# Retention attention followed by a GELU MLP on one core: the first unit's v over SyncE's queue, attention visits timed to TensorE's instruction pieces, and a new order of loads

## The chip, the core and the metric

The kernel runs on one core of a Trainium2 chip. TensorE (PE in the profile) multiplies, VectorE (DVE), ScalarE (ACT) and GpSimd (POOL) do the elementwise work, and the queues of SyncE (SP), ACT and POOL issue transfers to 16 shared DMA engines. The metric is the device time of one execution in microseconds; less is better.

## The reference

Inputs are q, k and v, each 8 x 8 x 576 x 64 fp32 (batch, heads, positions, width of a head), and two weights. The first part is attention without a softmax: each score is damped by a power of the head's gamma.

```python
scores = scale * np.matmul(q, k.transpose(0, 1, 3, 2))
Dmat = np.where(rel >= 0, gamma[:, None, None] ** rel[None, :, :], 0.0)
ret = scores * Dmat[None, :, :, :]
attn_out = np.matmul(ret, v)
x = attn_out.transpose(0, 2, 1, 3).reshape(4608, 512)
h = x @ w_in                      # w_in 512 x 2048
g = 0.5 * h * (1.0 + erf(h / sqrt(2)))
out = g @ w_out                   # w_out 2048 x 512
```

## The kernel before

**Units and visits.** The 576 positions are cut into chunks of 128 and a tail of 64. A unit is one chunk of one batch element with all 8 heads (the two tails of a pair of batch elements share one unit); there are 36. Units 0 to 3 stand alone, later chunks go in groups of two. A group passes these steps on PE: its q and k are transposed (`turn`, L421, by PE; from group 8 on `turn_dve`, L441, by DVE); a visit called S makes the scores (`scores`, L473, L488 to L506), and DVE multiplies them by the damping (`masked`, L527 to L533, tile `ret`); a visit called A (`attend`) multiplies by v (`inner`, L558 to L569), updates the state that a chunk hands to the next (`state`, U, L584, L589) and adds what the state before gives (`cross`, L646). DVE or ACT then writes the result into `x` (L669, L383). The first visit A, of unit 0, reads v as it was loaded.

**The MLP.** Four units make a block of 512 tokens; there are 9 blocks. `mlp1` (L689, tile `hT`) is the first product, followed by GELU on ACT into `g_all`; `mlp2` (L722, tile `oT`) is the second for half of block 0. The rest of the second product, and the first product of blocks 6 to 8, use Strassen-like schemes of seven products in place of eight (`mlp2_fast`, L793, tiles `fa`, `fb`; `mlp1_fast`, L897, tiles `ha`, `hb`), whose sums and differences DVE makes (`g_sum`, L761; the sums of the weights, L748 and L862).

**What sets the order.** The Python program is a planner. It keeps a clock for each engine in `T`, estimated landing times in `land`, and in its main loop picks the next piece of PE work: a due U, A, S or transposition first, else a step of the MLP. Dummy products (`warm`, L1112 and L1139) fill waits in the first 16 us. Loads come from the list `ORDER`, which POOL's queue issues one after the other (`load`: L322 for q, k, v, L278 for pieces of `w_in`, L293 for pieces of `w_out`); these convert fp32 to bf16 on the way, and eight semaphores go round, so that POOL holds back a load while the eighth before it is under way. After the list, `reload` adds loads as units are finished. Only unit 0's q and k come over SP's and ACT's queues (L132), as fp32, and are cast by DVE or ACT (L381, through `cast_due`). Constants of the planner: `RATE` bounds how far attention runs ahead of the MLP's block number, `SB` how much planned DVE work may be ahead when a visit S is let in, `PER_B` weighs the MLP's sums against attention's jobs on DVE, `STORE_AT` is the earliest time of block 0's stores, `CROWD` the time up to which a store is planned to delay loads, `STATE10` the earliest time of the state of units 2 and 3. In the planner as it stands, PE's clock knows nothing of the fetching of instructions.

Below are the functions that the diff touches and what calls them.

Of the kernel before, what the change touches and what calls it, by code (L numbers as in the profile page):

```python
# [17 lines left out]
def kernel(  # L18
# [72 lines left out]
    HK = N_DF // 2  # L91
# [181 lines left out]
    def load(what, i):  # L273
        if what == "io":
            constants()
            return
        if what == "wi":
            nc.gpsimd.dma_start(w_in[:, :, i * 256:(i + 1) * 256],  # L278
                                moe_w_in[:, i * 256:(i + 1) * 256].rearrange("(c p) f -> p c f", p=128))
            land_in[i] = sw_dma(0.75, 1.33)  # L280
            return
# [34 lines left out]
        for jj in (j,) if j is not None else range(2):  # L316
# [3 lines left out]
            else:  # L320
# [47 lines left out]
    def release(b, when):  # L368
        held.remove(b)
        free_at[b] = when  # L370

    def pe(dur, to="full"):
# [42 lines left out]
    def turn(n, jj, half):  # L415
        qk, dst = loaded[groups[n][0]][0][jj], turned(n, jj)
        b, t = bank([128, HP, 128], BF16, "qk_ps")
        rows = TAIL if units[groups[n][0]][2] is None else C
        for x in range(HP):
            what = qk[:, 2 * x:2 * x + 2, :] if n < 4 else qk[0:rows, HP * half + x, :, :]  # L420
            nc.tensor.transpose(t[:, x, 0:rows], what, ident[0:rows, 0, 0:rows])  # L421
# [42 lines left out]
    def scores(n):  # L464
# [3 lines left out]
        if n < 4:  # L468
            got = [bank([128, HP, 128], FP32, "sc") for _ in range(2)]
            for hp in range(HP):  # L470
                for e in range(2):
                    sl = slice(64 * e, 64 * e + 64)
                    nc.tensor.matmul(got[e][1][:, hp, :], lhsT=kT[sl, hp, :], rhs=qT[sl, hp, :],  # L473
                                     start=True, stop=True)
            st[g[0]]["sc"] = got, pe(0.23, "row")
        elif n in BY_DVE:
# [5 lines left out]
            for hp in range(HP):  # L482
                for y in range(2):
                    for e in range(2):
                        for j in range(2):
                            sl = slice(64 * e + 32 * j, 64 * e + 32 * j + 32)
                            dst = got[e][1][64 * j:64 * j + 64, hp, :] if short else got[j][e][1][:, hp, :]
                            nc.tensor.matmul(dst, lhsT=turned_k(n, sl, hp, y), rhs=turned_q(n, sl, hp, y),  # L488
                                             start=(y == 0), stop=(y == 1), skip_group_check=True)
# [3 lines left out]
        elif len(g) == 1:  # L493
            got = [bank([128, H, TAIL], FP32, "sc") for _ in range(2)]
            for h in range(H):
                for j in range(2):
                    sl = slice(64 * j, 64 * j + 64)
                    nc.tensor.matmul(got[j][1][sl, h, :], lhsT=kT[sl, h, :TAIL], rhs=qT[sl, h, :TAIL],
                                     start=True, stop=True)
            st[g[0]]["sc"] = got, pe(0.23, "quad")  # L500
        else:
            got = [[bank([128, HP, 128], FP32, "sc") for _ in range(2)] for _ in g]
            for h in range(H):
                for j in range(2):
                    sl = slice(64 * j, 64 * j + 64)
                    nc.tensor.matmul(got[j][h % 2][1][:, h // 2, :], lhsT=kT[sl, h, :], rhs=qT[sl, h, :],  # L506
                                     start=True, stop=True)
# [41 lines left out]
    def inner(i):  # L549
        bp, ci, j = units[i]  # L550
        s = st[i]
        if j is None:
            s["o"] = [bank([128, HP, TAIL], FP32, "o_ps") for _ in range(2)]
            for h in range(H):
                for jj in range(2):
                    sl, e = slice(64 * jj, 64 * jj + 64), 64 * (h % 2)
                    y = h // 2 + HP * (h % 2) if group_of[i] in BY_DVE else h
                    nc.tensor.matmul(s["o"][jj][1][e:e + 64, h // 2, :], lhsT=s["vh"][sl, h, :], rhs=s["ret"][0][sl, y, :],  # L558
                                     start=(h < 2), stop=False, skip_group_check=True)
            s["B"] = pe(0.25, "quad")  # L560
            s_done.add(i)
        else:
# [3 lines left out]
            for hp in range(HP):  # L566
                for z in range(4):
                    e, d0 = z // 2, z % 2 * 32
                    nc.tensor.matmul(o[32 * z:32 * z + 32, hp, :], lhsT=vals[:, 2 * hp + e, d0:d0 + 32], rhs=s["ret"][e][:, hp, :],  # L569
                                     start=(hp == 0), stop=(ci == 0 and hp == HP - 1), skip_group_check=True)  # L570
# [4 lines left out]
    def state(bp, ci):  # L575
        pair = pair_of[bp, ci]
        b, u_ps = bank([128, H, D], FP32, "u_ps")
        for hp in range(HP) if packed(pair[0]) else ():
            for y in range(2):
                for e in range(2):  # L580
                    for j, i in enumerate(pair):
                        h, p0 = 2 * hp + e, 64 * e + 32 * j
                        keys = loaded[i][0][1][:, h, y::2] if i < 4 else loaded[i][2][:, h, j, y::2]
                        nc.tensor.matmul(u_ps[p0:p0 + 32, 2 * hp + y, :], lhsT=keys, rhs=st[i]["vh"][:, h, :],  # L584
                                         start=(hp == y == 0), stop=(hp == HP - 1 and y == 1), skip_group_check=True)
        for h in range(H) if not packed(pair[0]) else ():
            for j, i in enumerate(pair):
                keys = loaded[i][0][1][:, h, :] if i < 4 else loaded[i][2][:, h, j, :]
                nc.tensor.matmul(u_ps[64 * j:64 * j + 64, h, :], lhsT=keys, rhs=st[i]["vh"][:, h, :],  # L589
                                 start=(h == 0), stop=(h == H - 1), skip_group_check=True)  # L590
# [36 lines left out]
    def cross(n):  # L627
# [7 lines left out]
        for hp in range(HP):  # L635
            for y in range(2) if by_dve else (None,):
                for e in range(2):
                    for j in range(2):
# [7 lines left out]
                        nc.tensor.matmul(o[64 * e:64 * e + 64, hp, :], lhsT=a, rhs=b_, start=False,  # L646
                                         stop=(hp == HP - 1 and y != 0), skip_group_check=True)
# [37 lines left out]
    def mlp1(t, m0, n, lo, hi):  # L685
        b, hT = bank([128, n, hi - lo], FP32, "hT")
        for m in range(m0, m0 + n):
            for cc in range(N_DM):
                nc.tensor.matmul(hT[:, m - m0, :], lhsT=w_in[:, cc, m * 128:m * 128 + 128], rhs=x_tiles[t][:, cc, lo:hi],  # L689
                                 start=(cc == 0), stop=(cc == N_DM - 1))  # L690
# [25 lines left out]
    def mlp2(t, ts, m0, m1):  # L716
# [4 lines left out]
        for m in range(m0, m1):  # L721
            nc.tensor.matmul(oT, lhsT=g_of(t, ts // 2)[:, m, cols], rhs=w_out[:, m, :], start=(m == 0), stop=(m == N_DF - 1))  # L722
        done = pe((m1 - m0) * 0.2158)
# [58 lines left out]
    def mlp2_fast(t, p, name):  # L782
# [9 lines left out]
        for kk in range(HK):  # L792
            nc.tensor.matmul(dst, lhsT=x[:, kk, :], rhs=y[:, kk, :], start=(name in "125" and kk == 0),  # L793
                             stop=(kk == HK - 1), skip_group_check=True)
# [85 lines left out]
    def mlp1_fast(t, i, name):  # L880
# [13 lines left out]
        for m in range(2):  # L894
            for cc in range(HC):
                c0 = (2 * i + m) * 128
                nc.tensor.matmul(dst[:, m, :], lhsT=a[cc][:, c0:c0 + 128], rhs=y[:, cc, :],  # L897
                                 start=(name in "125" and m == 0 and cc == 0), stop=(cc == HC - 1), skip_group_check=True)
# [210 lines left out]
    def warm(n):  # L1109
        b, t = bank([128, 512], FP32, "warm")  # L1110
        for _ in range(n):
            nc.tensor.matmul(t, lhsT=zeros[:, :128], rhs=zeros, start=True, stop=True)  # L1112
        pe((0.32 if T["pe"] < HOT else 0.2158) * n)
# [23 lines left out]
    for _ in range(N_WARM):  # L1137
        b, t = bank([128, 512], FP32, "warm")
        nc.tensor.matmul(t, lhsT=zeros[:, :128], rhs=zeros, start=True, stop=True)  # L1139
        release(b, 0.0)  # L1140
    T["pe"] = 1.3 + 0.62 * N_WARM
    while True:
# [16 lines left out]
        if nB < nA:  # L1159
# [109 lines left out]
```

## Time and profile before

| | |
|---|---|
| three runs, median (lowest to highest) | 292.16 us (291.55 to 292.23) |
| profiled execution, its own time | 292.13 us |
| its span | 290.3 us |
| outside the span | 1.83 us |
| PE busy | 284.0 us (98%), 3992 matmuls |
| DVE, POOL, ACT busy | 241.5, 159.4, 144.0 us |
| granted PE clock | 1.0 |
| PE's instructions, by their DMA queue q8 | 31 transfers of 16 KB |

A line of the timeline gives start, duration, engine, source line, operation, output<-input and, in brackets, how long the engine stood idle before it and what ended that. In the chain of waits each line is a piece of the path that ended last: start, duration, and what filled it. PE's busy time counts overlapping matmuls to their modelled ends, so that "busy" hides small gaps; spacings between starts show them. q8 carries PE's instructions in pieces of 16 KB: some 7,984 instructions (3992 weight loads and as many matmuls) in 31 pieces are 256 to a piece.

### The profile page before, as it was taken

How to read it: one execution, taken by the hardware profiler on the slowest of the kernel's cores; microseconds unless marked ns; L12 is line 12 of the kernel's file. 1: busy time of each engine (PE TensorE's matmuls, PEld its weight loads, DVE VectorE, ACT ScalarE, POOL GpSimd, SP SyncE). 2: the span in 40 equal slices, each digit the busy share in tenths (PEclk: the TensorE clock that was granted, in tenths of full speed). 3: DMA queues.
4: the chain of work that ended last, by engine and by line, in shares of the span. 5: the costliest groups of instructions: out<-in, count | busy, mean ns of one | idle time of the engine just before them, and what ended most of it. 6: DMA issues, size and time to landing. Idle time of an engine off the chain costs nothing.

```text
span 290.3 us, 9332 instructions
## 1 busy us (share of the span) xinstructions
PE 284.0 (98%) x3992; PEld 212.6 (73%) x3992; DVE 241.5 (83%) x445; ACT 144.0 (50%) x270; POOL 159.4 (55%) x232
## 2 busy tenths in 40 slices
PE   7999999999999999999999999999999999999995
PEld 2588677888874566666666676677888888888884
DVE  5581599789999999989983388999999998899962
ACT  7377333665346546555365544434545545543521
POOL 8975689999878898889799994300000000000000
PEclk9999999999999999999999999999999999999999
DMA  9999999999999999999999992002002101201013
GB/s 145 165 188 202 188 179 185 164 117 113 149 162 129 135 118 114 181 93 142 159 135 189 146 98 72 5 5 75 2 0 76 72 2 72 76 0 73 37 58 128
DMA packets 111418, 31.55 MB, mean 109 GB/s; under 512 B 89104, under 2 KB 107024, under 8 KB 111376
## 3 DMA queue, kind: packets, MB, share of 16 engines
q0 software_dynamic: 103744, 20.99, 85.0%
q1 hardware_dynamic: 6144, 9.18, 9.5%
q10 hardware_dynamic: 1488, 0.79, 1.0%
q8 instruction: 31, 0.51, 0.7%
q14 instruction: 11, 0.09, 0.1%
HBM read 42.47 MB, written 9.44 MB: 179 GB/s over the span
## 4 chain that ended last, share of the span: by engine, by line
PE 80%; DMA 9%; POOL 6%; DVE 4%; issue 1%; POOLq 0%; DVEq 0%
PE hT L689 23%; PE fa L793 19%; PE fb L793 14%; PE ha L897 7%; PE hb L897 5%; DMA w_out<-in_moe_w_out_dram 4%; DMA w_in<-in_moe_w_in_dram 3%; POOL early L322 3%; PE o_ps L569 3%; DMA qk_ld<-in_q_dram 3%; PE o_ps L646 2%; PE sc L488 2%; POOL w_in L278 2%; PE u_ps L584 1%; PE qk_ps L421 1%; DVE ret L533 1%
## 5 line engine op out<-in xcount | busy, mean ns | idle before, releaser
L689 PE MATMUL hT<-x,w_in 128*128 128x512 bf16 (+2 forms) x536 | 93.1, 319 | 0.1
L689 PEld LDWEIGHTS <-w_in 128*128 128x128 bf16 x536 | 48.8, 98 | 24.5 <-issue 0.3
L793 PEld LDWEIGHTS <-g_all 128*128 128x128 bf16 x544 | 52.3, 98 | 11.2 <-issue 1.1
L694 ACT ACTIVATE g_all<-hT 128x512 bf16<-128x512 f32 x64 | 38.2, 597 | 41.1 <-PE hT L689 41.1
L793 PEld LDWEIGHTS <-s 128*128 128x128 bf16 x408 | 39.6, 98 | 9.1 <-issue 0.6
L902 ACT ACTIVATE g_all<-t 128x512 bf16<-128x512 f32 x36 | 22.6, 630 | 32.9 <-DVE t L910 32.9
L306 POOL DMA_DIRECT2D k_ld<-in_k_dram x56 | 31.0, 568 | 8.5 <-DMA kn_ld<-in_k_dram 4.7
L533 DVE TENSOR_TENSOR ret<-sc,msk 128x512 bf16<-128x512 f32 x56 | 34.7, 681 | 1.0 <-PE sc L506 1.0
L779 DVE TENSOR_TENSOR o_sb<-fb,t 128x256 f32<-128x256 f32 x51 | 21.2, 418 | 17.1 <-ACT t L383 7.6
L793 PE MATMUL fa<-w_out,g_all 128*128 128x256 bf16 x272 | 35.1, 273 | 0.0
L322 POOL DMA_DIRECT2D v_ld<-in_v_dram x36 | 30.8, 858 | 2.5 <-DMA q_ld<-in_q_dram 1.4
L306 POOL DMA_DIRECT2D q_ld<-in_q_dram x56 | 31.1, 584 | 0.6 <-DMA qk_ld<-in_q_dram 0.6
L383 ACT COPY t<-fa 128x256 f32<-128x256 f32 x39 | 14.5, 371 | 29.5 <-PE fa L793 29.4
L910 DVE TENSOR_TENSOR t<-hb,t 128x512 f32<-128x512 f32 x36 | 24.7, 687 | 2.5 <-ACT t L383 1.5
L697 ACT ACTIVATE g_all<-hT 128x512 bf16<-128x512 f32 (+1 forms) x35 | 19.3, 560 | 10.8 <-PE hT L689 10.6
L669 DVE TENSOR_TENSOR x<-o_ps,dqT 128x512 bf16<-128x512 f32 (+1 forms) x36 | 20.9, 621 | 1.1 <-PE o_ps L646 1.1
L897 PEld LDWEIGHTS <-ws 128*128 128x128 bf16 x192 | 18.8, 98 | 2.5 <-issue 0.3
L312 POOL DMA_DIRECT2D kn_ld<-in_k_dram x22 | 19.9, 902 | 0.9 <-DMA q_ld<-in_q_dram 0.9
L793 PE MATMUL fb<-w_out,g_all 128*128 128x256 bf16 x136 | 17.7, 273 | 0.4 <-issue 0.4
L793 PE MATMUL fb<-w_out,s 128*128 128x256 bf16 x136 | 17.5, 273 | 0.3 <-DVE o_sb L779 0.3
L793 PE MATMUL fa<-wt,g_all 128*128 128x256 bf16 x136 | 17.5, 273 | 0.0
L793 PE MATMUL fa<-wt,s 128*128 128x256 bf16 x136 | 17.5, 273 | 0.0
(119 smaller groups left out, 453.0 us busy)
## 6 DMA issues: line engine op xcount, KB each, us to landing
out_dram<-o_sb SPq DMA_DIRECT2D x30, 256.0 KB, 2.8
v_ld<-in_v_dram POOLq DMA_DIRECT2D x28, 128.0 KB, 5.1
q_ld<-in_q_dram POOLq DMA_DIRECT2D x44, 64.0 KB, 4.4
k_ld<-in_k_dram POOLq DMA_DIRECT2D x44, 64.0 KB, 3.4
kn_ld<-in_k_dram POOLq DMA_DIRECT2D x22, 128.0 KB, 5.3
w_in<-in_moe_w_in_dram POOLq DMA_DIRECT2D x8, 256.0 KB, 6.9
w_out<-in_moe_w_out_dram POOLq DMA_DIRECT2D x8, 256.0 KB, 10.6
out_dram<-o_sb SPq DMA_DIRECT2D x7, 128.0 KB, 2.4
```

Source lines behind the costliest of these rows:

```text
L306: nc.gpsimd.dma_start(qk["qk".index(what)][p0:p0 + 32, 0:HP * per].rearrange("p (h x) -> p h x", h=HP), {"q": q, "k": k}[what][2 * bp + jj ...
L312: nc.gpsimd.dma_start(kn[:, :, j], k[2 * bp + j, :, ci * C:ci * C + C, :].rearrange("h s d -> s h d"))
L322: nc.gpsimd.dma_start(dst, src[2 * bp + jj, :, ci * C:ci * C + n, :].rearrange("h s d -> s h d"))
L533: nc.vector.tensor_tensor(r, t, by, op=ALU.mult)
L669: nc.vector.tensor_tensor(x[:, :, n * y:n * y + n], o, dqT[:, :, ci * C:ci * C + n], op=ALU.mult)
L689: nc.tensor.matmul(hT[:, m - m0, :], lhsT=w_in[:, cc, m * 128:m * 128 + 128], rhs=x_tiles[t][:, cc, lo:hi], start=(cc == 0), stop=(cc == N ...
L694: nc.scalar.activation(g_all[:, t % 2, :, m0, :], hT.rearrange("p n (a c) -> p (n a) c", a=2), AF.Gelu)
L779: nc.vector.tensor_tensor(dst, src, f[key], op=ALU.add)
L793: nc.tensor.matmul(dst, lhsT=x[:, kk, :], rhs=y[:, kk, :], start=(name in "125" and kk == 0), stop=(kk == HK - 1), skip_group_check=True)
L897: nc.tensor.matmul(dst[:, m, :], lhsT=a[cc][:, c0:c0 + 128], rhs=y[:, cc, :], start=(name in "125" and m == 0 and cc == 0), stop=(cc == HC ...
L902: nc.scalar.activation(g_of(t, part)[:, m0:m0 + 2], src, AF.Gelu)
L910: nc.vector.tensor_tensor(f[key], f["b"][1], f[key], op=ALU.add)
```

## The change

1. Unit 0's v is loaded at the start over SP's queue, behind q, as fp32 into a third tile (`first_v`), and cast like q and k through `cast_due`, with a planned landing at 7.45 us. The entry `v0` of `ORDER` then does nothing.
2. Every matmul and transposition goes through `mm` or `mm_turn`, which count PE's instructions. `pe()` notes when the count passes into a new piece of 256 and delays PE's planned clock if the piece before was passed less than `FETCH` = 5.0 us ago. `fetch_at` holds back visits A (192 instructions) and S (64) from group 4 on that would run into the next piece sooner than that.
3. `ORDER` is new in its first three quarters, and seven constants differ.

```diff
-    RATE = 4.6
-    STORE_AT = 48.0
-    CROWD = 66.0
-    STATE10 = 24.0
+    RATE = 3.8
+    STORE_AT = 58.0
+    CROWD = 40.0
+    STATE10 = 20.0
     HOT = 7.5
-    SLACK, SB, PER_G, PER_B, TURN0 = 1.6, 9.0, 6.0, 40.0, 3.0
+    FETCH = 5.0
+    SLACK, SB, PER_G, PER_B, TURN0 = 1.6, 12.0, 6.0, 30.0, 3.0
...
+    V0_HW = 1
...
-    for nm, src, eng in (("q32", q, nc.sync), ("k32", k, nc.scalar)):
+    for nm, src, eng in (("q32", q, nc.sync), ("k32", k, nc.scalar), ("first_v", v, nc.sync))[:2 + V0_HW]:
...
+        if what == "v" and i == 0 and V0_HW:
+            return
...
+    if V0_HW:
+        land["v", 0] = 7.45
...
-    ORDER = ("wi0 io k2 k1 v1 q1 v0 wi1 q2 q3 k3 wi4 v2 wi6 v3 wi7 wi5 wo2 wi3 wi2 wo0 wo3 wo1 wo6 k4 wo4 wo5 wo7 "
-             "q5 q4 k5 k6 q6 k7 v4 v5 q7 v8 v7 k9 dq2 v6 v9 q9 k8 q8 dq3 q11 v11 k10 q10 q12 dq4 v10 k12 n12 v12 "
+    if V0_HW:
+        cast_due["v", 0] = (loaded[0][1], first["first_v"])
+    ORDER = ("wi0 io k1 v1 q1 k2 wi1 q2 v0 wi4 q3 k3 v2 wi6 wo0 v3 wi5 wi7 wo2 wi3 wi2 wo3 wo6 wo1 k4 wo4 wo5 k5 "
+             "wo7 q5 q4 q6 k7 v4 k6 v5 q7 v8 v7 q9 k9 dq2 q8 v6 v9 k8 dq3 q11 v11 n12 k10 q12 k12 q10 dq4 v10 v12 "
              "n11 dq0 k11").split()
...
+    count = [3.0, 3.0]
+    piece = [0.0]
+
+    def mm(*a, **k):
+        count[0] += 2.004
+        nc.tensor.matmul(*a, **k)
...
+    def place(n):
+        return (n - 194.0) // 256, (n - 194.0) % 256
+
+    def fetch_at(n):
+
+        at = place(count[0])[1]
+        wait = piece[0] + FETCH - (256 - at) * 0.0075 if at + n >= 256 else 0.0
+        return 0.0 if T["pe"] < 20.0 else wait
...
     def pe(dur, to="full"):
...
-        T["pe"] += dur * (2.0 if T["pe"] < HOT else 1.0)
+        dur *= 2.0 if T["pe"] < HOT else 1.0
+        new, old = place(count[0])[0], place(count[1])[0]
+        if new > old:
+            turn_at = T["pe"] + dur * (1 - place(count[0])[1] / max(1.0, count[0] - count[1]))
+            wait = max(0.0, piece[0] + FETCH - turn_at) if T["pe"] > 20.0 else 0.0
+            piece[0] = turn_at + wait
+            T["pe"] += wait
+        count[1] = count[0]
+        T["pe"] += dur
...
-            acts.append((max(ready, free_time(out_banks(g))), "A"))
+            acts.append((max(ready, fetch_at(192 if n >= 4 else 0), free_time(out_banks(g))), "A"))
...
-                acts.append((max(sg[n]["T"], free_time(2 * len(g))), "S"))
+                acts.append((max(sg[n]["T"], fetch_at(64 if n >= 4 else 0), free_time(2 * len(g))), "S"))
```

More of the change, by code (lines that the diff above doesn't have):

```diff
@@ L370, in release, with mm_turn, one_piece @@
         free_at[b] = when
+    count = [3.0, 3.0]
[3 more added lines that the diff above has]
+        nc.tensor.matmul(*a, **k)
+    def mm_turn(*a, **k):
+        count[0] += 2.004
+        nc.tensor.transpose(*a, **k)
+    def place(n):
[4 more added lines that the diff above has]
+        return 0.0 if T["pe"] < 20.0 else wait
+    def one_piece(n):
+        return place(count[0])[1] + n < 512
     def pe(dur, to="full"):
@@ L420, in turn @@
             what = qk[:, 2 * x:2 * x + 2, :] if n < 4 else qk[0:rows, HP * half + x, :, :]
-            nc.tensor.transpose(t[:, x, 0:rows], what, ident[0:rows, 0, 0:rows])
+            mm_turn(t[:, x, 0:rows], what, ident[0:rows, 0, 0:rows])
         done = pe(0.225)
@@ L472, in scores @@
                     sl = slice(64 * e, 64 * e + 64)
-                    nc.tensor.matmul(got[e][1][:, hp, :], lhsT=kT[sl, hp, :], rhs=qT[sl, hp, :],
+                    mm(got[e][1][:, hp, :], lhsT=kT[sl, hp, :], rhs=qT[sl, hp, :],
                                      start=True, stop=True)
@@ L497, in scores @@
                     sl = slice(64 * j, 64 * j + 64)
-                    nc.tensor.matmul(got[j][1][sl, h, :], lhsT=kT[sl, h, :TAIL], rhs=qT[sl, h, :TAIL],
+                    mm(got[j][1][sl, h, :], lhsT=kT[sl, h, :TAIL], rhs=qT[sl, h, :TAIL],
                                      start=True, stop=True)
@@ L505, in scores @@
                     sl = slice(64 * j, 64 * j + 64)
-                    nc.tensor.matmul(got[j][h % 2][1][:, h // 2, :], lhsT=kT[sl, h, :], rhs=qT[sl, h, :],
+                    mm(got[j][h % 2][1][:, h // 2, :], lhsT=kT[sl, h, :], rhs=qT[sl, h, :],
                                      start=True, stop=True)
@@ L557, in inner @@
                     y = h // 2 + HP * (h % 2) if group_of[i] in BY_DVE else h
-                    nc.tensor.matmul(s["o"][jj][1][e:e + 64, h // 2, :], lhsT=s["vh"][sl, h, :], rhs=s["ret"][0][sl, y, :],
+                    mm(s["o"][jj][1][e:e + 64, h // 2, :], lhsT=s["vh"][sl, h, :], rhs=s["ret"][0][sl, y, :],
                                      start=(h < 2), stop=False, skip_group_check=True)
@@ L568, in inner @@
                     e, d0 = z // 2, z % 2 * 32
-                    nc.tensor.matmul(o[32 * z:32 * z + 32, hp, :], lhsT=vals[:, 2 * hp + e, d0:d0 + 32], rhs=s["ret"][e][:, hp, :],
+                    mm(o[32 * z:32 * z + 32, hp, :], lhsT=vals[:, 2 * hp + e, d0:d0 + 32], rhs=s["ret"][e][:, hp, :],
                                      start=(hp == 0), stop=(ci == 0 and hp == HP - 1), skip_group_check=True)
@@ L645, in cross @@
                             a, b_ = u[sl, 2 * hp + e, :], turned(n, 0)[sl, 2 * hp + e, cols]
-                        nc.tensor.matmul(o[64 * e:64 * e + 64, hp, :], lhsT=a, rhs=b_, start=False,
+                        mm(o[64 * e:64 * e + 64, hp, :], lhsT=a, rhs=b_, start=False,
                                          stop=(hp == HP - 1 and y != 0), skip_group_check=True)
@@ L688, in mlp1 @@
             for cc in range(N_DM):
-                nc.tensor.matmul(hT[:, m - m0, :], lhsT=w_in[:, cc, m * 128:m * 128 + 128], rhs=x_tiles[t][:, cc, lo:hi],
+                mm(hT[:, m - m0, :], lhsT=w_in[:, cc, m * 128:m * 128 + 128], rhs=x_tiles[t][:, cc, lo:hi],
                                  start=(cc == 0), stop=(cc == N_DM - 1))
@@ L721, in mlp2 @@
         for m in range(m0, m1):
-            nc.tensor.matmul(oT, lhsT=g_of(t, ts // 2)[:, m, cols], rhs=w_out[:, m, :], start=(m == 0), stop=(m == N_DF - 1))
+            mm(oT, lhsT=g_of(t, ts // 2)[:, m, cols], rhs=w_out[:, m, :], start=(m == 0), stop=(m == N_DF - 1))
         done = pe((m1 - m0) * 0.2158)
@@ L792, in mlp2_fast @@
         for kk in range(HK):
-            nc.tensor.matmul(dst, lhsT=x[:, kk, :], rhs=y[:, kk, :], start=(name in "125" and kk == 0),
+            mm(dst, lhsT=x[:, kk, :], rhs=y[:, kk, :], start=(name in "125" and kk == 0),
                              stop=(kk == HK - 1), skip_group_check=True)
@@ L1111, in warm @@
         for _ in range(n):
-            nc.tensor.matmul(t, lhsT=zeros[:, :128], rhs=zeros, start=True, stop=True)
+            mm(t, lhsT=zeros[:, :128], rhs=zeros, start=True, stop=True)
         pe((0.32 if T["pe"] < HOT else 0.2158) * n)
@@ L1138 @@
         b, t = bank([128, 512], FP32, "warm")
-        nc.tensor.matmul(t, lhsT=zeros[:, :128], rhs=zeros, start=True, stop=True)
+        mm(t, lhsT=zeros[:, :128], rhs=zeros, start=True, stop=True)
         release(b, 0.0)
```

8 lines of the change are left out of this document (4 added, 4 removed).

## The prediction

> **What bounds the kernel now.** First the page's busy times and its chain of waits:
>
> ```profile
> PE 284.0 (98%) x3992; PEld 212.6 (73%) x3992; DVE 241.5 (83%) x445; ACT 144.0 (50%) x270; POOL 159.4 (55%) x232
> PE 80%; DMA 9%; POOL 6%; DVE 4%; issue 1%; POOLq 0%; DVEq 0%
> ```
>
> PE is the bound, but 15% of the chain is POOL and DMA. The same chain in order of time shows where:
>
> ```profile
> 2.65 4.37 POOL early L322 x5
> 7.01 0.75 POOL w_in L278
> 7.77 2.63 POOL early L322 x3
> ...
> 15.74 9.03 DMA w_in<-in_moe_w_in_dram
> 25.05 10.60 DMA w_out<-in_moe_w_out_dram
> ...
> 37.77 7.36 DMA qk_ld<-in_q_dram
> 45.18 1.07 PE qk_ps L421 x16
> ```
>
> Up to 45.18 us the end is set by POOL issuing loads one by one, then by transfers; from there PE leads. The third view, the timeline, shows the start of PE and POOL and two later places where PE stands still:
>
> ```profile
> 6.10 0.91 POOL L322 DMA_DIRECT2D early<-in_v_dram  x1
> 7.77 3.85 PE L1112 MATMUL warm<-zeros 128*128 128x512 bf16 x10
> 12.43 0.41 PE L569 MATMUL o_ps<-ret,early 128*32 128x128 bf16 x16
> ...
> 139.71 1.03 PE L689 MATMUL hT<-x,w_in 128*128 128x512 bf16 x4
> 141.15 1.05 PE L793 MATMUL fb<-w_out,g_all 128*128 128x256 bf16 x8 [0.42 <-issue]
> ...
> 178.28 1.03 PE L793 MATMUL fb<-w_out,s 128*128 128x256 bf16 x8 [0.28 <-DVE o_sb L779]
> ```
>
> The first visit A waits for v0, fifth in POOL's queue, while PE runs dummies. At 141.15 PE waits for nothing that the profile names; in the queues' view a transfer of q8 (PE's instructions) lies between 138.1 and 140.0. Four hT there took 1.44 us from start to next start, 0.87 elsewhere: 0.57 lost. The fourth view, busy time by stage, says what runs beside PE:
>
> ```profile
> 60.00:100.00 40.00, 40.00 (x773) 29.06 (x772) 39.16 (x66) 21.73 (x39) 35.59 (x57) 1.00 1.39 136
> 100.00:140.00 40.00, 40.00 (x765) 26.28 (x763) 38.25 (x65) 20.39 (x37) 36.56 (x57) 1.00 1.37 131
> ```
>
> The columns are PE, weight loads, DVE, ACT, POOL: from 60 to 140 us DVE is full too (39.2 and 38.3 of 40).
>
> **The change, part by part.** The sum is made against the profiled execution's 292.13 us (span 290.3, 1.83 around it), 0.03 under the median.
>
> *v0 off POOL's queue.* It removes one of ten issues of L322 in the chain (5+3+1+1), 4.37/5 = 0.87 to 0.91 us; what follows v0 up to q7, the load that ends the chain at 45.18, moves by 0.9. Can PE follow? v0 being there by 8, A0 can run near 9.4 instead of 12.43, and q1 (now fourth of POOL's loads) comes 0.9 earlier; then by 14.4 PE can have done, over what it has now, the second visit A (0.34 from start to next start), the first state (0.38) and three more first products of 128 tokens (0.45 each): 2.07, say 2.0 us, for which the dummies (3.85 us at 7.77) make room. But PE then reaches the end of its work sooner: the eight products of oT end at 38.84, and by the trace's semaphores the last piece of w_out, which they need, lands at 36.65. In the new order k5 goes before it (+0.9) and v0 is gone (-0.9), so it stays, and oT can end no earlier than 36.65 + 0.86 (four 0.216 us products) = 37.5, 1.3 before now. Ends: -2.0 (all of PE's early work kept) and 0 (transfers alone set the chain). I take -0.9, the POOL row, between oT's -1.3 and 0.
>
> *v0 on SP's queue.* 256 KB as fp32; q, alike, lands in 3.6 us, at 4.3; k on ACT at 4.9. The three move at 204 to 288 GB/s in the timeline of transfers, so v0 costs the DMA engines 262 KB / 0.25 = 1.05 us, POOL's bf16 v0 131 KB / 0.16 = 0.8. Net +0.2; ends 0 and +1.05, if k and the first w_in come later by all of it. A late k delays the transposes of 5.70, covered by the dummies; without them 1.05. The cast (0.43, row of q's) falls into DVE's idle 0.77 before 7.94. SP's issue (0.44) is ahead of nothing: its first store is at 39.
>
> *Pieces.* Visits that would run into the next piece are held back. Seen stalls: 0.57 at 141; the other visible waits of PE after 45 name DMA (0.3) or DVE (0.3). Ends: -1.5 (unnamed starts of 0.1 after some 15 visits in one) and 0. I take -0.57, the row. The hold itself stops nothing on PE, since the planner issues an MLP step instead; behind the held visit wait DVE's ret and x and the next state. At the worst it is 5.0 - 192 x 0.0075 = 3.56 us after a turn of pieces; in 100 to 200 us PE has a block or more of second product in hand (14 products of 0.87 = 12 us), so it costs 0 there. Without that cover it costs what it holds. The Trainium skill (Runtime: NRT & Kernel Launch, Instruction fetch mechanics) says that the sequencer fetches the next block of 256 instructions while it executes the current one, and that this is mostly hidden; by it the term is 0 and the sum -0.7, by the row -0.57 and -1.27. The trace agrees in 30 of 31 pieces, not at 141.
>
> *Orders and constants.* wo0 comes 6 places earlier (one piece, some 1.3 us of transfer, ahead of v3, wi5, wi7); PE has hT to do at 20 to 32 (64 products from 25.79): 0. k2 later: needed only with q2. State (1,0) at 20: its 0.35 us of PE are only moved. Stores at 58: two o_sb of four stay held from 39, the next second product starts at 68: 0, and loads from 48 to 58 have less beside them. RATE: at 122 us attention is at unit 24 and the MLP at block 3.56, where the limit was 32.4 and is 29.5: not reached. SB and PER_B change DVE's order; S behind A saves PE a change of shape (32 `sc` take 0.38 at 95.91, 0.56 at 84.47, so 0.18), and there are 14 such visits: five more or fewer of these savings are -0.9 to +0.9, I take 0.
>
> Sum: -0.9 + 0.2 - 0.57 = -1.27: 290.86, so 290.9.
>
> **The rivals.** *All of PE's start is kept* (289.1): -2.0 in place of -0.9, pieces -0.57, the 0.44 at 178 (1.31 against 0.87 for four hT) and the 0.26 at 45 go, with the +0.2 it is -3.07. For it: PE waits 3.85 us in dummies. Against: w_out's landing allows 1.3.
>
> *DVE takes it back* (291.6). DVE writes block 2's x from 83.64 to 84.90, and its first hT starts at 84.98, behind a visit S, just as block 1's second product runs out. A PE that is 0.7 earlier by 60 would stand there unless DVE, full since 60, is earlier as well; DVE idles 2.7 us from 50 to 60, which speaks for it. Only the pieces stay: 292.13 - 0.57.
>
> *Slower: DVE's queue* (293.9). SB lets a visit S in behind 12 planned us of DVE work instead of 9, so one more visit's four ret (2.48 us at 171.99) can stand ahead of sums that the second product waits for. PE can put 4 hT and 8 f (1.73) in between, so such a case costs 0.75. Before has one, at 178 (0.44). Nine visits S of L488 lie between 60 and 140, where DVE is full; from three on it outweighs the forecast's gain (3 x 0.75 against 1.27 + 0.88); four give -1.27 + 3.0.
>
> *The holding back does nothing* (291.4): pieces arrive in time whatever the planner does, the 0.57 was something else, and only -0.7 stays. For it: pieces passed in 3.7 us at 96 to 99.7 cost under 0.1 by the spacings. Against: the transfer that ends just before PE goes on. It is the rule of the Trainium skill's page named above.
>
> **How the numbers follow.** The measurement tells 0.3% (0.88 us): faster is under 291.28, slower over 293.04. Forecast 0.40 (290.0 to 291.6; 0.36 faster, 0.04 same); all kept 0.16 (faster); DVE takes it back 0.12 (0.02, 0.07, 0.03 slower); DVE's queue 0.26 (slower); hold does nothing 0.06 (0.02, 0.03, 0.01). Together faster 0.56, same 0.14, slower 0.30. The range 288.6 to 294.0 leaves out the lower third of the second case (0.05) and the upper half of the fourth (0.12).
>
> **What would show it.** v0 right: the first o_ps of L569 near 9.4 to 10.5, one L322 fewer in the chain, the q7 transposes near 44.5. SP's v wrong: k's cast well after 4.92. Pieces right: no "issue" idle of PE over 0.2 after 20 us. RATE right: the last visit A near 197 as now (196.67). DVE's queue: PE idle before fa or fb released by DVE sums between 60 and 200, and spans of hT and f unchanged otherwise. The prediction is wrong if PE, early at 45, has lost it at 85, or if visits end after 200 and block 6's sums (ws, L862, 5.5 us of DVE) then come late.

## Result and the profile after

The changed kernel is slower: 301.01 us (median of four runs, 300.63 to 301.6) against 292.2 of the kernel before on the same chip, a ratio of 1.0311 with an interval of 1.0283 to 1.0339. The forecast was 290.9, and 301 lies above its range. The profiled execution took 301.25 us with a span of 299.5: 9.12 us longer than the profiled execution of the kernel before. Ratios in this document leave out executions more than 1.5% above the fastest of their kernel, and those can be the very ones with a held sum, so for after_no_fetch and after_vh_gap the median over all executions says more.

The page of the changed kernel: busy times, the granted clock in 40 slices, and the shares of the chain.

```profile
PE 282.0 (94%) x3988; PEld 213.3 (71%) x4012; DVE 246.4 (82%) x444; ACT 145.4 (49%) x275; POOL 158.9 (53%) x231
PEclk9999999999999999999999998999999999999999
PE 52%; DMA 21%; POOL 13%; DVE 9%; issue 4%; ACT 0%; POOLq 0%; ACTq 0%; DVEq 0%
```

PE has the same work (a few of its records are missing) and 98% has become 94%; DVE's share of the chain has gone from 4% to 9%, and one slice, the 25th (180 to 187 us), has a lower clock than the rest. The changed kernel's chain in order of time (start, duration, what filled it):

```profile
2.64 3.68 POOL early L326 x4
...
16.48 10.71 DMA w_in<-in_moe_w_in_dram
28.36 9.00 DMA w_out<-in_moe_w_out_dram
37.64 8.36 DMA qk_ld<-in_q_dram
46.04 1.07 PE qk_ps L390 x16
...
74.37 2.39 DVE ret L573 x4
...
173.33 7.78 DVE s L801
184.20 1.02 PE sc L386 x30
```

The start still ends in the same load, q7, but 0.86 us later (46.04 against 45.18). One line is new and larger than any cost that the prediction weighed: 7.78 us of a single DVE sum at 173.33. Busy time by stage (PE, weight loads, DVE, ACT, POOL, clock, DMA share, GB/s) shows the same place:

```profile
60.00:100.00 40.00, 39.03 (x761) 28.14 (x761) 38.34 (x64) 22.08 (x40) 37.29 (x59) 1.00 1.35 123
100.00:140.00 40.00, 39.07 (x728) 26.29 (x736) 38.53 (x66) 20.20 (x37) 35.02 (x55) 1.00 1.35 138
170.00:180.00 10.00, 9.36 (x123) 6.28 (x123) 9.96 (x7) 2.83 (x6) 9.78 (x13) 1.00 0.48 40
180.00:190.00 10.00, 5.96 (x143) 4.24 (x144) 9.56 (x16) 3.00 (x7) 1.60 (x2) 0.83 0.12 26
```

From 170 to 180 DVE is busy for 9.96 of 10 us with seven instructions, and in the next ten PE works 5.96 us, at a clock of 0.83. The timeline there, put together from its rows for DVE, POOL, ACT and PE:

```profile
173.25 7.85 DVE L801 TENSOR_TENSOR s<-g_all 128x1024 bf16<-128x1024 bf16 x1
173.41 7.13 POOL L582 TENSOR_TENSOR vh<-v_ld,dv 128x512 bf16<-128x512 bf16 x7
182.35 0.68 DVE L634 CAST u_sb<-u_ps 128x512 bf16<-128x512 f32 x1
183.07 0.59 ACT L636 COPY u_acc<-u_ps 128x512 f32<-128x512 f32 x1 [7.57 <-DVE u_sb L634]
183.71 0.21 PE L386 MATMUL sc<-q_ld,kT 32*128 32x128 bf16 x1 [4.29 <-ACT u_acc L636]
185.16 1.89 PE L386 MATMUL fa<-wt,g_all 128*128 128x256 bf16 x8
```

Read from the top: a sum of two bf16 tiles, 0.68 us elsewhere, takes 7.85, as long as POOL's run of seven `vh` products (v times a factor per head, `scaled_v`, which units from `VH_POOL` = 26 on do on POOL), and ends 0.56 after that run. Behind it in DVE's queue stands the cast of the state `u_sb`, behind that ACT's copy of the same bank of PSUM, and a visit S on PE waits 4.29 us for the bank. PE takes its work in the program's order here: the MLP work behind the visit stands as well, and no matmul starts between 179.4 and 183.7. After the stop eight `fa` take 1.89 us, 1.03 elsewhere.

How far PE's work is behind that of the kernel before can be followed through the whole trace: each matmul is counted by its usual spacing, and the lag is how much later the same amount of work is done (23 records missing in the changed kernel's trace are put in their places; single values depend on how that is done, by up to 0.5 us). The columns are times of the kernel before: what it has done at 180 the changed kernel has done at 188.4.

| PE's lag, us, at | 20 | 40 | 50 | 80 | 100 | 140 | 150 | 170 | 180 | end |
|---|---|---|---|---|---|---|---|---|---|---|
| changed kernel | -1.1 | 0.1 | 0.8 | 1.4 | 1.7 | 2.0 | 1.2 | 2.1 | 8.4 | 8.3 |

6.3 us go between 170 and 180, at the sum. Another 0.8 comes after the start of PE's last matmul (4.57 us to the end of the span, 3.75 before; the last store lands 2.8 us after its issue, 1.7 before). The remaining 2 are small steps, most of them named in the waits of PE in the changed kernel (total, times, longest):

```profile
PE sc L386 <- ACT u_acc L636: 4.3, 1, 4.3
PE qk_ps L390 <- DMA early<-in_q_dram: 1.3, 1, 1.3
...
PE qk_ps L390 <- DMA qk_ld<-in_q_dram: 1.0, 1, 1.0
PE o_ps L386 <- POOL vh L582: 0.8, 1, 0.8
PE o_ps L386 <- DVE vh L582: 0.6, 1, 0.6
PE fa L386 <- ACT t L423: 0.5, 1, 0.5
```

### The profile page after: what moved, and what is told of

It reads as the page before. It is cut to its first block, busy times and chain, and to the rows that moved or that the text cites. A ratio compares the mean times of both kernels' runs of the same rounds, so it can differ in the third digit from the quotient of the medians.

```text
span 299.5 us, 9348 instructions
## 1 busy us (share of the span) xinstructions
PE 282.0 (94%) x3988; PEld 213.3 (71%) x4012; DVE 246.4 (82%) x444; ACT 145.4 (49%) x275; POOL 158.9 (53%) x231
## 4 chain that ended last, share of the span: by engine, by line
PE 52%; DMA 21%; POOL 13%; DVE 9%; issue 4%; ACT 0%; POOLq 0%; ACTq 0%; DVEq 0%
PE fa L386 12%; PE hT L386 11%; PE fb L386 10%; DMA kn_ld<-in_k_dram 8%; PE ha L386 7%; PE hb L386 5%; PE o_ps L386 4%; DVE s L801 4%; DMA w_in<-in_moe_w_in_dram 4%; DMA v_ld<-in_v_dram 3%; POOL v_ld L326 3%; DMA w_out<-in_moe_w_out_dram 3%; DMA qk_ld<-in_q_dram 3%; POOL early L326 3%; POOL k_ld L310 2%
## 5 line engine op out<-in xcount | busy, mean ns | idle before, releaser
L386 PE MATMUL hT<-x,w_in 128*128 128x512 bf16 (+2 forms) x538 | 90.7, 310 | 1.4 <-issue 0.3
L386 PEld LDWEIGHTS <-w_in 128*128 128x128 bf16 x704 | 63.1, 98 | 26.4 <-DMA w_in<-in_moe_w_in_dram 0.4
L386 PEld LDWEIGHTS <-g_all 128*128 128x128 bf16 x576 | 56.0, 98 | 15.5 <-issue 0.8
L326 POOL DMA_DIRECT2D v_ld<-in_v_dram x36 | 30.7, 856 | 1.4 <-DMA w_out<-in_moe_w_out_dram 0.7
L801 DVE TENSOR_TENSOR s<-g_all 128x1024 bf16<-128x1024 bf16 x17 | 19.6, 1155 | 8.6 <-ACT g_all L737 8.6
L386 PE MATMUL fa<-wt,g_all 128*128 128x256 bf16 x136 | 18.3, 281 | 0.5 <-ACT t L423 0.5
```

The costliest lines, as they stand in the source:

```text
L326: nc.gpsimd.dma_start(dst, src[2 * bp + jj, :, ci * C:ci * C + n, :].rearrange("h s d -> s h d"))
L386: nc.tensor.matmul(*a, **k)
L801: nc.vector.tensor_tensor(s[i], x, y, op=op)
```

## Experiments

The theory: a sum on DVE whose inputs are both in SBUF is held while POOL's `vh` products run back to back, and the change moved a sum into the start of a longer run. The rivals: the hold-back of visits costs the time by itself; the new loads do; the 7.85 us are a reading of the trace and PE waits for something else. Where an expectation names a theory by a letter, A is the collision and the others are rivals, each with its numbers. Ratios are to runs of the kernel before on the same chip, whose medians were 292.2 to 293.5. A lag is from one execution and can differ by about 1 us in another, since single waits for loads and instructions do.

**1. POOL's products on DVE, all else in its place.** In the changed kernel and in the one before:

```diff
-        (nc.gpsimd if on_pool else nc.vector).tensor_tensor(vh, ...
+        nc.vector.tensor_tensor(vh, ...
```

> The changed kernel, with the products vh of units 26 to 35 issued on DVE in the same place of the program where they went to POOL; the order of everything else is the same. Theory A (the run of seven vh on POOL holds one DVE sum for 7.85 us, and that sum holds PE): the 6.3 us that PE falls behind between 170 and 185 shrink to 0 to 2, the time is 294.5 to 297. Rival B (visits stand ahead of inputs that are late anyway, the long sum is only where it shows): the loss stays, 300 to 302.

> The kernel before with the same edit. Theory A: its run of five vh costs little (two DVE sums 2.2 us longer, PE 0.44), so the time is 291.5 to 293. Rival B: also no change beyond 0.5. A time over 294 would say that DVE can't take the ten products (6.8 us) at all, and then the run above can't tell A from B.

Measured: the changed kernel falls from 301.0 to 294.53, ratio 1.0045 (1.0009 to 1.0081); its lag is 2.25 at 170, 2.09 at 180 and 2.77 at the end, so the step of 6.3 is gone though DVE has ten products more. The kernel before comes to 294.65, ratio 1.0034 (1.0003 to 1.0066), a miss: it was expected at 291.5 to 293, and over 294 the pair was not to tell A from B. What tells them apart is the changed kernel itself, which B had at 300 to 302. The collision is the cause of most of the loss. In their old places POOL's products are worth about 1 us to the kernel before: they are only harmful where they meet the sum badly.

**2. What the hold depends on.** First, more of POOL's work at the same place: each of its products issued twice, in the kernel before and in the changed one.

```diff
+        for _ in range(2 if on_pool else 1):
             (nc.gpsimd if on_pool else nc.vector).tensor_tensor(vh, ...
```

> The kernel before with every vh on POOL issued twice, one behind the other, so that its run of five becomes ten; nothing else differs. Theory A (a DVE sum of two SBUF tensors that meets the run waits for nearly all the rest of it): one sum of 5 to 9 us in place of 2.05, PE stopped for 3 to 7, a granted clock below 0.995 in every execution, 296 to 301. Rival E (the sums don't wait for the run; only the visits that need vh come later by up to 5 us): all sums stay under 2.1 us, PE fills with the MLP, 292 to 294.

> The changed kernel with each of POOL's vh products issued twice; nothing is left out. Gap theory (in the kernel before, with the products issued twice, the second of each pair began some 0.08 us after the first ended, and no sum took over 1.6 us in a run of 16): the sum at 173 takes under 2.1 us although POOL's work doubles, time 294 to 297, with up to 1 us of PE waiting for vh. Strict theory: 14 products in the place of seven, the sum is held for 13 to 16 us, PE stands for 9 or more, time above 304.

The kernel before came to 293.08, ratio 1.0007 (0.9979 to 1.0036): 16 products in a row cost nothing, and in the profiled execution no sum took over 1.54 us. The changed one came to 297.64 (294.76 to 300.74), ratio 1.016 (1.0086 to 1.0235), faster than with half the products. The timeline of its profiled execution, the fastest (294.76; the other three took 297.5 to 300.7, and no trace shows what their sums did):

```profile
173.96 18.49 POOL L583 TENSOR_TENSOR vh<-v_ld,dv 128x512 bf16<-128x512 bf16 x16
174.14 1.51 DVE L802 TENSOR_TENSOR s<-s,g_all 128x1024 bf16<-128x1024 bf16 x1
175.57 1.54 DVE L802 TENSOR_TENSOR g_all<-g_all 128x1024 bf16<-128x1024 bf16 x1
```

Here the sums beside a run of 18 us wait for one product each, not for the run. So the strict form (a sum waits for the whole run, however it came to meet it) fell. In these two kernels the second product of a pair starts 0.08 us after the first ends, while the products of the changed kernel's run start 0.04 to 0.07 before the record of the one ahead ends. The next guess was therefore that a gap lets the sum in:

```diff
         (nc.gpsimd if on_pool else nc.vector).tensor_tensor(vh, ...
+        if on_pool:
+            gap = vh_pool.tile([128, 1], FP32, tag="gap", name="gap")
+            nc.gpsimd.memset(gap, 0.0)
```

> The changed kernel with one tiny fill of a 128x1 tile put on POOL behind each of POOL's vh products; nothing is left out. Gap theory (a sum of two SBUF tiles that arrives on DVE during a back-to-back run on POOL is held to about the run's end; a short stretch of POOL that doesn't read SBUF lets it in): the sum that took 7.85 us at 173 takes under 2.5 us, the 8.6 us by which PE's work stands behind the kernel before at the end shrink to 2 to 3.5, time 294 to 296. Strict theory (the sum waits for the run whatever stands between): the run is as long and so is the hold, time 299 to 302. If the fill itself costs more than 0.3 us, POOL's later products are late by the sum of the fills, and the visits that need vh show waits on POOL; that is told by PE's waits.

The median is 302.35 (three runs at 302.3 to 303.6, one at 297.07). What was expected of the fill fell, in the timeline as in the time:

```profile
174.21 8.00 DVE L804 TENSOR_TENSOR s<-g_all 128x1024 bf16<-128x1024 bf16 x1
175.30 0.11 POOL L585 MEMSET gap<- 128x1 f32 x1
175.36 1.06 POOL L582 TENSOR_TENSOR vh<-v_ld,dv 128x512 bf16<-128x512 bf16 x1
```

A fill between the products leaves the sum held to the end of the seventh. But with the fill the starts still overlap (the product at 175.36 begins before the fill's record ends), so POOL is never idle there, and whether a real gap lets the sum in is not shown. Then a shorter run, by every second product on DVE:

```diff
-        (nc.gpsimd if on_pool else nc.vector).tensor_tensor(vh, ...
+        (nc.gpsimd if on_pool and i % 2 else nc.vector).tensor_tensor(vh, ...
```

> The changed kernel with every second one of POOL's ten vh products issued on DVE in its old place, so that the run of seven on POOL becomes one of three or four; nothing is left out. Theory that the hold lasts as long as the run does: the sum that took 7.85 us takes 3 to 4.5, DVE has 3 or 4 products of 0.68 more, PE's work 4 to 6.5 us behind the kernel before at the end, time 296.5 to 299, between the changed kernel (301.0) and the one with all of them on DVE (294.5). Rival, that any run starts the hold and its end is set by something else on POOL: 299 to 302. Rival, that products on DVE between the sums make the two engines take turns: no sum over 1.6 us, 294.5 to 296.

294.99, ratio 1.0066 (1.0034 to 1.0099), below the 296.5 to 299 expected and within what the third case was given, though a sum did wait. The run became two, and the sum beside it was held for just these two, timeline:

```profile
171.37 2.86 DVE L801 TENSOR_TENSOR s<-g_all,s 128x1024 bf16<-128x1024 bf16 x1
171.59 2.08 POOL L582 TENSOR_TENSOR vh<-v_ld,dv 128x512 bf16<-128x512 bf16 x2
174.48 0.68 DVE L801 TENSOR_TENSOR s<-g_all 128x1024 bf16<-128x1024 bf16 x1
```

2.86 is 2.18 more than the sum's 0.68, for a run of 2.08; 7.85 is 7.17 more, for one of 7.13. A hold of two products costs PE 0.7 us of lag between 170 and 180, one of seven 6.3: the shorter hold seems to be covered in greater part by the work that PE has ahead.

**3. One part of the change at a time,** POOL's products as they were.

```diff
+    V0_HW = 1                      # v0_only: the kernel before with the earlier v
```
```diff
-    ORDER = ("wi0 io k2 k1 ...     # order_only: the kernel before with the new list
+    ORDER = ("wi0 io k1 v1 ...
```
```diff
+    FETCH = 5.0                    # fetch_only: the kernel before with the hold-back
```
```diff
-        return 0.0 if T["pe"] < 20.0 else wait      # after_no_fetch: the changed kernel without it
+        return 0.0
...
-            wait = max(0.0, piece[0] + FETCH - turn_at) if T["pe"] > 20.0 else 0.0
+            wait = 0.0
```

> The kernel before with only v0 over SP's queue as fp32; the old list of loads and the old constants. Theory C (the transfers, not POOL's issues, set when loads land from the first on, and v0 as fp32 costs them 1 us): w_in's first piece lands 0.5 to 0.8 later than 6.72, q1 and all that follows lands within 0.5 of before although it is issued 0.9 earlier, the q7 transposes start at 44.7 to 45.7; visit A of unit 0 comes 1.5 to 2 earlier and that lead is gone by 40 us. Rival D (the prediction's: POOL's issues set it): q7 0.7 to 0.9 earlier, PE 0.5 to 0.9 ahead at 50. Time by C 291.5 to 293.5, by D 290.8 to 292, both without the accident of vh, which adds 3 to 6.

> The kernel before with only the new list of loads (v0 over POOL, at its new place, after q2). Theory C: the last piece of w_out lands about 0.9 later than 36.65 because k5 goes before it, so PE is 0.5 to 1 behind at 50 us, and the first visit A is 1 to 2 later; 293 to 295. Rival D: the list alone is worth nothing without v0 on SP; within 0.5 of before at 50. The accident of vh adds 3 to 6 if it strikes.

> The kernel before with only the hold-back for pieces. If the hold-back costs by itself: over 295, with PE falling behind in the dense visits of 70 to 140 and 180 to 200. If it does what it says: 291.6 to 292.2 and no gap at a turn of pieces. The accident of theory A can strike here too; it shows as one DVE sum of over 4 us beside a run of vh.

> The changed kernel without the hold-back: the wait for pieces is 0 in the planner's clock and in the visits. If the hold-back is what makes it slow: 291 to 293.5. If order and constants do: 299 to 302. If it is the accident of where POOL's vh and DVE's sums meet (theory A), PE is 0.5 to 2 us behind before 170 as in the changed kernel, and the rest depends on the run of vh in the trace: 0 or 4 to 6 us more, 293 to 300.

| kernel | us, median | ratio (interval) | lag at 50 | 80 | 170 | 180 | end |
|---|---|---|---|---|---|---|---|
| v0_only | 298.36 | 1.0169 (1.0081 to 1.0257) | 0.9 | 2.1 | 2.3 | 5.1 | 5.0 |
| order_only | 296.57 | 1.0094 (1.0048 to 1.014) | 0.8 | 2.8 | 2.9 | 4.2 | 3.9 |
| fetch_only | 294.9 | 1.004 (1.0002 to 1.0078) | -0.1 | -0.1 | 0.0 | -0.6 | 1.8 |
| after_no_fetch | 296.38 | 1.0052 (1.0003 to 1.0102) | | | 0.0 | 4.5 | 5.4 |

No part alone gains. Not all of these losses are the collision: in order_only's profiled execution no sum beside POOL's products takes over 1.43 us, and PE stands 0.46 and 1.03 us at 76 and 78 (for `t` and `o_sb`) and 1.18 at 177 (for `g_all`); fetch_only's 1.8 comes after 200, where PE waits for `ws` and `t`, up to 0.75 us. The hold-back is not the cause of the 6.3: without it the collision is still there in the profiled execution (a run of five; the sum takes 4.69 us), and PE's timeline has

```profile
182.11 1.34 PE L386 MATMUL fb<-w_out,s 128*128 128x256 bf16 x8 [3.76 <-DVE o_sb L819]
```

v0_only shows the other way in which the two can meet. A sum was still in progress when the run began, and from then on they took turns, timeline:

```profile
171.47 0.68 DVE L801 TENSOR_TENSOR s<-g_all 128x1024 bf16<-128x1024 bf16 x1
171.91 6.99 POOL L582 TENSOR_TENSOR vh<-v_ld,dv 128x512 bf16<-128x512 bf16 x5
172.19 1.43 DVE L801 TENSOR_TENSOR s<-s,g_all 128x1024 bf16<-128x1024 bf16 x1
173.54 1.54 DVE L801 TENSOR_TENSOR g_all<-g_all 128x1024 bf16<-128x1024 bf16 x1
```

Five products take 6.99 us here and 5.59 in the kernel before, each sum about 0.8 more than its 0.68, and PE loses 2.8 in all. Which of the two happens seems to vary between executions of one kernel (after_no_fetch ran from 292.58 to 299.26), but only one execution of each was traced.

**4. The parts without the collision.** With `VH_POOL` = 36 the planner itself gives all `vh` to DVE and orders its work by that.

```diff
-    VH_POOL = 26
+    VH_POOL = 36
```

> The kernel before with VH_POOL at 36 and nothing else: base for the run without the hold-back (291.75). If taking vh off POOL is all that made that run fast: 291.3 to 292.2 here too, in a spread of under 1 us and no clock under 0.997. If list, constants and v0 give something as well: 292.2 to 293.5.

> The changed kernel with VH_POOL at 36: the planner itself gives all vh to DVE, and counts their time there, so the order of visits from 140 us on is another. Theory A: no DVE sum over 2 us, no loss at 170 to 185; PE 1.5 to 3 behind before at the end, 293 to 296. Rival B: loss of over 4 us stays somewhere between 140 and 200, since DVE has too much to do; 297 or more.

> The same with the hold-back for pieces taken out as well: v0 on SP, the new list and the new constants stay. Theory A with the hold-back as the second cost (1 to 1.5 us between 90 and 170): 291.5 to 293.5, and no execution with a granted clock of 0.994 or less, because that clock comes from PE's stop behind the long sum. If the hold-back helps: later than the run before it by 0.5 or more.

> The kernel before with VH_POOL at 36 and the new constants; old list, v0 on POOL, no hold-back. If the constants are what gains: 0.5 to 1.5 under the run before it. If they are worth nothing: within 0.5 of it.

> New list and new constants, VH_POOL at 36, no hold-back, v0 over POOL at its place in the new list: only v0 differs from the run of 291.75. Theory C (v0 on SP gives no load earlier): the same within 0.5 at the end, since the lead of visit A is gone by 40 us. Rival D: 0.7 to 1.5 slower without it.

> The kernel before with the first unit's v alone over SyncE's queue and all vh products on DVE; old order of loads and work, old constants, no hold-back. Nothing is left out. Theory that the collision is most of what this part lost alone (298.4 with POOL's products, PE's work 2.3 us behind at 150, 5.1 at the end): now 293.5 to 295.5, PE's work 1 to 2.5 us behind at the end and no sum on DVE over 2 us. Rival, that the later loads are what it loses (wi0 0.88 us later, q1 0.7 later): 295.5 to 297.5.

> The best kernel so far (first unit's v over SyncE's queue, new order, new constants, no hold-back, all vh on DVE: 291.75) with the old constants. Nothing is left out. Theory that it gains by the pair of v and order, and the constants are worth nothing: 291.3 to 292.5. Rival, that the constants (fewer credits, a longer lead for the sums) bring the visits of the later groups early and carry the gain: 293 to 294.5, PE's work 1 us or more behind from 140 on.

> The same kernel as the best one so far (first unit's v over SyncE's queue, new order and constants, no hold-back, all vh on DVE), once more on another occasion, since it was the best of many and may owe part of that to luck. If its gain is real: ratio to the kernel before 0.993 to 0.998, 291 to 292.5 and no run above 293. If it was luck: 0.999 to 1.004.

| kernel (all vh on DVE) | early v | order | constants | hold-back | us | ratio (interval) | lag at end |
|---|---|---|---|---|---|---|---|
| before_vhpool36 | | | | | 292.88 | 0.9998 (0.9966 to 1.003) | |
| v0_vh36 | x | | | | 293.87 | 1.0065 (1.0042 to 1.0087) | 3.0 |
| const_vh36 | | | x | | 293.88 | 1.0037 (1.0005 to 1.007) | 1.7 |
| v0_order_vh36 | x | x | | | 294.12 | 1.0075 (1.0048 to 1.0103) | 2.1 |
| no_v0_vh36 | | x | x | | 293.36 | 1.003 (1.0003 to 1.0056) | 0.8 |
| no_fetch_vh36 | x | x | x | | 291.75 | 0.9951 (0.992 to 0.9982) | -0.3 |
| no_fetch_vh36_again | x | x | x | | 291.82 | 0.997 (0.9953 to 0.9988) | -0.5 |
| after_vhpool36 | x | x | x | x | 294.06 | 1.0015 (0.9975 to 1.0055) | 2.0 |

Early v and constants are each worth nothing or less by themselves (the order alone was run only with POOL's products, order_only), and the three gain together: no_fetch_vh36 beats the kernel before, on two occasions, by 0.3 to 0.5% and with all 22 of its runs between 291.5 and 292.4. The two guesses that a part could be left out of it both missed: leaving out the constants costs 2.3 us (294.12; by the rival's expectation, not the theory's), leaving out the early v 1.6, both measured on other chips; by the ratios it is 3.1 to 3.6 and 1.8 to 2.3. The hold-back then costs 2.3 (294.06 against 291.75). PE's lag between these two traces rises mainly in three steps: about 0.7 from 90 to 100, 0.8 from 140 to 150, 0.5 from 170 to 180. At the first two PE waits 0.59 for `vh` (100.14) and 0.48 for `u_sb` (142.87), which it doesn't without the hold-back.

## Why the prediction was wrong

**The step that failed is one that it doesn't have: where POOL's `vh` products fall beside DVE's sums.** It put nothing on this, and it cost 6.3 us. Rows of the timeline of the kernel before told of it:

```profile
171.75 5.59 POOL L542 TENSOR_TENSOR vh<-v_ld,dv 128x512 bf16<-128x512 bf16 x5
174.38 2.05 DVE L761 TENSOR_TENSOR g_all<-g_all 128x1024 bf16<-128x1024 bf16 x1
176.35 1.54 DVE L761 TENSOR_TENSOR s<-g_all,s 128x1024 bf16<-128x1024 bf16 x1
```

Beside a run of five products stand a sum of 2.05 and one of 1.54 where 0.68 is usual; the prediction took PE's short wait behind them, 0.28 at 178.28, as a case of a full DVE queue. The parts of the change only move work by a microsecond or two, and that decides whether a sum arrives within the run (before: 2.05), as its start is near (after: 7.85), or is already in progress (v0_only: turns). The rival "DVE's queue" had the right engine and sign, but not the mechanism or the place: it put 0.75 on a case and wanted three between 60 and 140; one case at 173 cost 6.3.

**Cover.** The hold-back was costed at 0 because 12 us of second product are in hand between 100 and 200. At the held sum none of it covered PE's wait: what stood at the head of PE's queue was a visit S whose PSUM bank hung behind the held sum, and the eight `fa` came after it. Whether they could have run earlier is not shown. Work in hand covers a wait only if it is ahead of the waiting instruction.

**v0 off POOL's queue, -0.9: not gained; with the new list PE is 0.8 behind at 50.** One L326 fewer stands in the chain, and the first visit A is at 10.61, as forecast (9.4 to 10.5, just over). PE was 1.1 ahead at 20 us and level at 40: the lead ended where the transfers do. q1 was issued 0.87 earlier and landed 0.09 earlier (10.24); q7, issued 0.13 earlier, landed 0.86 later (45.99). The term took the time of issue for the time of landing. In these traces the later q7 goes with the new list, not with the early v: it landed at 45.81 and 45.98 in order_only and no_v0_vh36, which have the list without the early v, and at 44.51 and 44.94 in v0_only and v0_vh36, which have the early v without the list. It isn't steady either: with the start of the kernel before it landed from 44.46 (before_vh_dve) to 46.09 (before_vhpool36), where the kernel before had 45.13. So the 0.8 is no more than one execution can differ from another.

**v0 on SP's queue, +0.2: too small.** The first piece of w_in landed 0.70 later (7.38 against 6.68), q and k 0.37 and 0.45 later. The upper end of 1.05 was the nearer one for these first loads; what that is worth in the total is not shown. Alone, without the new order, early v loses 0.65% (v0_vh36): k1 lands at 9.45 where it was 8.57, but q7 0.19 earlier, and PE's longest wait after the start is 1.08 us for `x` at 50.80.

**Pieces, -0.57: the stall goes, the hold costs more.** At 141 the changed kernel stands no more, and regains 0.8 there (lag 2.0 at 140, 1.2 at 150), 0.57 of it the stall of before. But visits moved by the hold wait for DVE elsewhere; in all the hold-back costs 2.3 us beside no_fetch_vh36, and 0.4% alone. That it cost nothing was the error; that pieces can be late was not. The rule of the Trainium skill (Runtime: NRT & Kernel Launch, Instruction fetch mechanics) that fetching is mostly hidden holds on the whole in these traces, with two exceptions, the 0.57 of before and the trace of before_vhpool36. There PE stood 1.58 us at the same turn of pieces (its weight loads have 2.1 us of "issue" there, and a transfer of q8 ends 1.3 us before PE goes on), nearly three times the 0.57, so the size of such a stall seems to vary between executions.

**Orders and constants, 0.** The rival's case came once: at 74.37 four `ret` stand ahead of what `fa` waits for, and PE loses 0.84 between 75 and 77 (0.75 had been put on it). It isn't the constants alone that bring it, since v0_vh36, with the old ones, has a wait of 0.46 at the same place. Constants without the rest cost 1.56 us of lag at 60; with early v and the new order they gain 2.3. Terms of a planner's kernel did not add up: the sum over parts was the wrong form.

**Clock.** That PE's clock would fall was not considered. After the stop it was 0.5 from 184.3 to 187.6 us (0.83 on average from 180 to 190), which adds about 0.9 us at eight `fa` alone (1.89 for 1.03).

## What to carry to other kernels

Before work is moved in a full schedule, look for the places where two engines use the same memory at once, and price them by the slowest row there (2.05 where 0.68 is usual), not by the mean: a shift of a microsecond can turn a row of 2 into one of 8. Ask what is at the head of the bound engine's queue when a wait comes, not how much work it has in hand. And where a planner orders the whole program, test parts together as well as alone: here none gained alone, and three gained together once the collision was out.

## What the runs showed of the hardware

**A sum on DVE beside products on POOL.** With both inputs in SBUF, a sum of 0.68 us took 2.86 beside a run of two products, 4.69 beside one of five and 7.85 and 8.00 beside runs of seven, when its record began 0.02 to 0.22 us ahead of the run's. Arriving inside a run of five it took 2.05 (before) and 3.21 (fetch_only). Each of these sums ends 0.55 or 0.56 us after the end of one product. In the runs of two and seven that is the last one; in the three runs of five it is the fourth, and the fifth then takes 1.52 to 1.55 instead of 1.07. So a sum isn't always held to the end of the run. With a sum begun 0.44 us or more ahead of the run (v0_only, after_vh_twice) the engines took turns: 1.43 to 1.54 for a sum, 1.39 to 1.50 for a product (1.07 alone). Instructions of DVE that read PSUM (`ret`, 0.68) ran beside the products at their usual time. The Trainium skill (SBUF — State Buffer, Who interferes with whom) says that a DVE instruction with two SBUF inputs contends with a GpSimd instruction that reads SBUF. It also says (SBUF — State Buffer, SBUF: two separate sides) that whichever starts first gets the shared ports for the whole instruction while the other blocks. The traces agree on which instructions contend; but if the ports went to the waiting engine at the end of an instruction, a sum would wait for one product, some 1.07 us, and here it waited for up to seven. What decides between waiting out products and taking turns is not settled: not the number of products (16 cost nothing) and not a fill of 0.1 us between them; a product that writes the same tile as the one ahead goes with turns in two kernels, but v0_only has turns without it.

**PE's clock after a stop.** After 4.29 us without a matmul the granted clock was 0.5 from 184.3 to 187.6 us. It fell in the same way after 3.76 us in after_no_fetch, and not after the 2.44 us for which PE stood in v0_only. The Trainium skill (TensorE: Matmul & The Clock Gate, What's actually happening) puts the return to the throttled state after an idle window of about 3.4 us, and the trace agrees.
